# Gateloop attention and a gated feed-forward on one core: the last steps of the range check placed among the last unit's output products

## The chip, the cores and the metric

The kernel runs on one core of a Trainium2 chip. The metric is the device time of one execution, in microseconds (us); the time shown is the median of three runs.

## The reference

Four batches, eight heads, 768 time steps, 48 channels a head. The first block is a recurrence over time with a complex gate; its result goes straight into a feed-forward block with 384 inputs, 2,048 hidden channels and 384 outputs, for 3,072 tokens.

```python
mag = np.sqrt(a_re * a_re + a_im * a_im)
scale = np.minimum(mag, 0.999) / (mag + 1e-06)
for t in range(S):
    new_re = ar * S_re - ai * S_im
    new_im = ar * S_im + ai * S_re
    kv = np.einsum('bhd,bhe->bhde', k[:, :, t], v[:, :, t])
    S_re, S_im = (new_re + kv, new_im)
    y[:, :, t] = np.einsum('bhd,bhde->bhe', q[:, :, t], S_re)
...
h = x @ w_in
sp = np.maximum(h, 0.0) + np.log1p(np.exp(-np.abs(h)))
out = (h * erf(sp)) @ w_out
```

## The kernel before

The work is cut into twelve units of 256 tokens (two chunks `c` of 128). For each unit the kernel takes logarithms and angles of the gates, sums them over time by a product with a triangular matrix, turns and scales `k` and `q`, forms scores and results of the recurrence, and sends the result through the feed-forward: `h` by products with `w_in` (L1178), a copy of `h` by ScalarE (L1181), softplus as a chain of exponentials and logarithms on ScalarE (L786, L787; L786 loads a function table), the Gelu and four VectorE instructions of `erf_times_h` (L1207 to L1213), and the output products (L1271). The weights arrive as 64-bit numbers and are narrowed by VectorE at the start (L844 to L849); later the same weights are loaded a second time and only looked at for small values (`look`, L859).

From the fourth unit on, the output product is done by a scheme with seven products in place of eight (`ff_out_7`). For a unit it makes the products X, Y, Z and W in this order; VectorE first builds sums of `h` (L1224, L1226, L1282, L1286) and of the weights (`sums_of_weights`, L894), and then reads each product into the output tile (L1279, L1291). After Z is read, the rows of the second half of the unit are stored (`put`, L1238), and after W the rows of the first half. Both stores are issued on SP's queue.

This fast way of computing, `quotient_path`, is only valid inside limits. So the kernel collects sums, maxima and minima while it runs, and `check` turns them into one number `ok`. `check` has three steps: the column sums on VectorE (L1337 to L1340), a small product on TensorE that adds over the 128 partitions (L1343), and six comparisons with limits and their minimum on VectorE (L1347, L1348). Then every engine loads `ok` into a register and branches over a second, general path (`product_path`) if it is 1:

```python
        yield
        within = const.tile([1, n], FP, name="within")
        for i, limit in enumerate(LIMITS):
            vector.tensor_scalar(out=within[:, i:i + 1], in0=ps[0:1, i:i + 1], scalar1=limit, scalar2=None, op0=OP.is_le)
        vector.tensor_reduce(out=ok, in_=within, axis=mybir.AxisListType.X, op=OP.min)
...
        fine = nc.values_load(ok[0:1, 0:1], min_val=0, max_val=1)
        with tc.If(fine < 1, label="general"):
            product_path(tc, q, k, v, a_re, a_im, w_in, w_out, out)
```

The load is L1424, the branch L1425. What every engine does after the branch is put down to L1425 and L1452: it checks that its own work is done, SP checks all the DMAs and then all engines, and a closing handshake follows.

The order of the work is written out by hand. `ORDER` is a list of 2,277 names; each name is a generator, and each time the name stands in the list its next step is issued (`next(steps[nm])`), on whichever engine's queue that step belongs to. Each engine works through its own queue in order. The names that this text speaks of: `t`, `l`, `m` the gates' logarithms, `e11.1.4` the steps of `erf_times_h` for unit 11, slab 1, channels 4 and 5 (Gelu, then the four VectorE instructions of which the last writes `h`), `b` sums of the weights, `i` the second look at the weights, `K` and `Q` the turning of `k` and `q`, `f` sums of `h`, `O11.0` to `O11.13` the output products of unit 11 with their reads and stores (`O11.4` and `O11.5` end X, `O11.7` ends Y, `O11.11` ends Z, `O11.13` ends W), and `Z` the three steps of `check`.

Of the kernel before, what the change touches and what calls it, by code (L numbers as in the profile page):

```python
# [49 lines left out]
u4_18 u4_2 u8_0 g0.0 g0.0 g0.1 g0.1 H u4_19 m0.0 m0.0 m0.0 m0.1 m0.1 t0.0 t0.0 l0.0 l0.0 l0.0 l0.0 m0.1 l0.0 p0.0  # L50
t0.1 t0.1 l0.1 l0.1 l0.1 p0.0 p0.0 u2_22 u8_1 n0 t0.0 t0.1 o0.1 l0.1 l0.1 o0.0 r0.0 n0 n0 n0 a0.0 a0.0 a0.0
u2_41 u2_34 q0.0 Q0.0 n1 n1 n1 r0.1 s0.0 s0.0 s0.0 Q0.0 u2_21 u2_39 a0.1 p0.1 u2_40 qT0.0.0 qT0.0.1 k0.0 K0.0
K0.0 kT0.0.0 kT0.0.1 u4_38 g1.0 t1.0 a0.1 g1.0 t1.0 p0.1 m1.0 qT0.0.1 m1.0 qT0.0.0 a0.1 p0.1 s0.1 s0.1 s0.1
u2_20 t1.0 kT0.0.0 kT0.0.1 o1.0 r1.0 n1 A0.0.0 A0.0.1 g1.1 m1.1 p0.0 A0.0.0 q0.1 Q0.1 v0.0 A0.0.1 n3 n3 S0.0
m1.0 a1.0 l1.0 Q0.1 qT0.1.0 k0.1 a1.0 K0.1 qT0.1.0 l1.0 p0.1 p0.0 S0.0 g1.1 qT0.1.1 qT0.1.1 l1.0 m1.1 K0.1 Y0.0
n3 l1.0 a1.0 l1.0 n3 kT0.1.0 kT0.1.1 n2 m1.1 kT0.1.0 A0.1.0 n2 p1.0 A0.1.0 t1.1 kT0.1.1 t1.1 Y0.0 t1.1 l1.1 p1.0
l1.1 p1.0 s1.0 l1.1 s1.0 s1.0 q1.0 v0.1 A0.1.1 A0.1.1 l1.1 n2 Q1.0 o1.1 l1.1 n2 r1.1 Y0.1 Y0.1 Q1.0 S0.1 S0.1 n4
n4 n4 p0.1 S0.1 n4 p1.1 p1.1 g2.1 g2.0 m2 g2.0 g2.1 m2 m2 n6 n6 k1.0 K1.0 qT1.0.0 qT1.0.0 qT1.0.1 a1.1 a1.1 p1.1
a1.1 t2 v1.1 K1.0 l2 t2 l2 h0.0.6 h0.0.6 l2 q1.1 t2 n6 Q1.1 p1.0 n7 n6 n7 k1.1 n5 g3.0 o2 l2 h0.0.4 h0.0.4 n7 l2
# [5 lines left out]
K2.0 Y1.0 Y1.1 t3 t3 S1.1 Y1.0 h1.0.0 K2.0 o3 S1.1 n10 K2.0 S1.1 S2.0 l3 h0.1.4 l3 r3 a3.0 l3 l3 n10 h1.0.2 S2.0  # L65
n12 l3 a3.0 a3.0 p2.0 S2.0 g4.0 g4.0 k2.1 K2.1 n10 g4.1 K2.1 q3.0 g4.1 M2.0 a3.1 a3.1 x0.0 h1.0.0 x0.0 e0.0.2
n12 e0.0.0 p3.1 p3.0 p3.1 p3.1 h1.1.0 M2.0 h1.0.2 M2.0 M2.0 p3.0 Q3.0 e0.0.0 n15 q3.1 v2.1 a3.1 e0.0.2 e0.0.0 m4
p3.0 h1.1.0 t4 e0.0.2 e0.0.0 e0.0.2 K2.1 a3.1 a3.1 Q2.1 g5.1 M2.1 p3.0 M2.1 k3.0 M2.1 p3.1 M2.1 p3.0 h1.1.6
e0.0.4 e0.0.4 h1.1.6 e0.0.6 e0.0.6 e0.0.4 e0.0.6 e0.0.4 m4 m4 e0.0.4 h0.1.2 A2.0.0 A2.0.1 n12 e0.0.6 n12 e0.0.6
A2.0.0 h0.1.2 s3 s3 s3 Q3.0 n15 K3.0 n14 k3.1 h1.0.4 x0.1 t4 x0.1 l4 x0.1 l4 h1.0.4 n15 K3.0 h1.0.6 x0.1 l4  # L70
A2.0.1 t4 n15 l4 O0.1 O0.0 O0.2 O0.4 O0.6 O0.3 A2.1.0 A2.1.0 A2.1.1 A2.1.1 e0.1.2 o4 l4 K3.0 e0.1.2 e0.1.0
e0.1.0 h1.0.6 r4 h1.1.4 h1.1.4 e0.1.2 Y2 Y2 Y2 a4.0 v3.0 e0.1.0 e0.1.2 a4.0 e0.1.0 e0.1.2 e0.1.0 e0.1.6 e0.1.6
e0.1.4 e0.1.4 e0.1.6 e0.1.4 Q3.0 e0.1.4 Q3.1 n14 h1.1.2 h1.1.2 a4.0 a4.0 a4.0 e0.1.6 Q3.1 K3.1 g5.1 x1.0 x1.0
p3.1 n13 x1.0 g5.0 g5.0 M3.0 a4.1 O0.5 O0.7 p4.0 h2.0.2 S3.0 e0.1.4 S3.0 n14 a4.1 n14 n13 e0.1.6 p4.0 p4.0 x1.0
v4.1 n13 n13 O0.9 O0.8 p4.1 p4.1 e1.0.0 h2.0.2 e1.0.0 e1.0.0 e1.0.2 e1.0.2 e1.0.0 e1.0.2 e1.0.0 e1.0.2 e1.0.2
k4.0 q4.0 v4.0 M3.0 a4.1 h2.1.2 M3.0 M3.0 O0.11 m5 h2.1.2 a4.1 m5 m5 K3.1 Q3.1 K3.1 h2.0.6 e1.0.4 h2.0.6 e1.0.4
e1.0.6 e1.0.6 e1.0.4 e1.0.6 l5 t5 p4.1 l5 t5 t5 l5 e1.0.4 Q4.0 p4.1 p4.1 M3.1 M3.1 M3.1 M3.1 q4.1 v3.1 x1.1
h2.0.0 h2.0.0 x1.1 O0.10 A3.0.1 A3.0.0 O0.13 O0.15 O0.12 O0.15 p4.0 p4.0 O0.15 h2.0.4 e1.0.6 e1.0.6 o5 e1.0.4
O0.14 l5 l5 A3.0.1 A3.0.0 l5 x1.1 O0.14 O1.0 x1.1 l5 a4.1 a5.0 A3.1.0 A3.1.0 A3.1.1 A3.1.1 e1.1.0 e1.1.0 e1.1.0
e1.1.2 e1.1.2 e1.1.2 j e1.1.2 e1.1.0 e1.1.2 e1.1.0 s4 s4 s4 Q4.0 r5 a5.0 O1.2 O1.4 O1.1 O1.6 e1.1.6 e1.1.6  # L80
e1.1.4 e1.1.4 e1.1.4 e1.1.6 e1.1.6 e1.1.4 e1.1.4 Y3 Y3 Y3 h2.0.4 x2.0 x2.0 a5.0 x2.0 h2.1.4 h2.1.4 x2.0 S3.1
h2.1.0 O1.3 K4.0 K4.0 K4.0 e1.1.6 S3.1 a5.0 S3.1 Q4.0 Q4.1 Q4.1 O1.8 S4.0 S4.0 S4.0 k4.1 K4.1 O0.14 M4.0 M4.0
e2.0.2 e2.0.2 M4.0 e2.0.0 e2.0.0 e2.0.2 M4.0 e2.0.0 v5.1 e2.0.2 p5.0 p5.0 p5.0 h2.1.6 h2.1.6 e2.0.2 e2.0.0
e2.0.0 e2.0.4 h2.1.0 e2.0.4 e2.0.4 e2.0.6 e2.0.6 e2.0.6 e2.0.6 O1.10 O1.12 a5.0 a5.0 a5.0 K4.1 p5.1 O1.14 p5.1
x2.1 x2.1 O1.5 O1.7 O1.9 K4.1 e2.0.4 a5.1 a5.1 p5.1 x2.1 Q4.1 a5.1 a5.1 A4.0.1 A4.0.1 e2.0.6 x2.1 A4.0.0 h3.0.2
# [9 lines left out]
e3.1.0 M5.1 M5.1 p6.1 O2.10 O2.12 p6.0 p6.1 p6.0 O2.15 p6.1 h4.0.0 h4.0.0 p6.0 e3.1.4 e3.1.4 O2.14 p6.1 g7.1  # L95
g7.1 p6.0 g7.0 b6 s6 e3.1.6 e3.1.4 e3.1.6 e3.1.6 Q6.0 e3.1.4 b2 b0 b2 b2 e3.1.6 g7.0 i0 M5.1 h4.0.4 h4.0.4 O2.14
i1 q6.1 s6 h4.1.6 s6 h4.1.6 m7 m7 m7 b0 l7 t7 l7 A5.0.1 A5.0.1 e3.1.6 Q6.0 i0 b4 e3.1.4 f3.1 b4 h4.0.6 h4.0.2 l7
l7 b4 i1 h4.0.2 h4.0.6 t7 b0 x4.0 A5.0.0 A5.0.0 A5.1.1 O3.0 O3.1 O3.2 h4.1.2 A5.1.0 h4.1.4 O3.3 x4.0 l7 l7 x4.0
x4.0 b2 b6 K6.0 K6.0 O3.1 O3.6 t7 b6 o7 A5.1.0 A5.1.1 Y5 l7 a7.0 e4.0.2 e4.0.2 e4.0.0 e4.0.0 e4.0.2 e4.0.2
e4.0.0 e4.0.2 e4.0.0 h4.1.2 r7 e4.0.0 e4.0.6 O3.2 e4.0.6 h4.1.4 k6.1 v6.0 O2.15 e4.0.4 e4.0.4 e4.0.6 e4.0.4 f3.1  # L100
h4.1.0 Y5 Y5 h4.1.0 O2.14 K6.0 e4.0.6 Q6.0 e4.0.4 x4.1 x4.1 x4.1 M6.0 M6.0 v7.1 M6.0 M6.0 O3.4 O3.5 O3.5 O3.5
O3.5 a7.0 e4.0.6 e4.0.4 a7.0 x4.1 h5.0.6 O3.7 O3.7 Q6.1 O3.7 a7.0 h5.0.2 Q6.1 K6.1 O3.4 e4.1.0 O3.8 e4.1.0 O3.12
a7.0 a7.0 a7.0 a7.1 v7.0 p6.0 e4.1.2 e4.1.2 e4.1.0 e4.1.0 e4.1.2 e4.1.0 e4.1.2 p7.1 h5.0.6 p7.1 p7.1 e4.1.2
e4.1.4 O3.9 O3.10 e4.1.6 p7.0 p7.0 p7.0 h5.0.2 e4.1.4 e4.1.4 e4.1.6 e4.1.6 O3.13 A6.0.1 O3.11 A6.0.0 O3.13 g8.0
# [4 lines left out]
A6.1.1 A6.1.1 h5.1.0 e5.0.4 e5.0.6 e5.0.6 e5.0.6 Q7.0 e5.0.4 Q7.0 O4.4 e5.0.6 e5.0.4 e5.0.6 e5.0.4 e5.0.4 h5.1.0  # L109
K7.0 h5.1.6 l8 l8 h5.1.6 l8 l8 l8 v6.1 Y6 Y6 x5.1 v8.0 x5.1 Y6 x5.1 l8 x5.1 O4.6 O4.7 S6.1 O4.7 O4.7 K7.0 K7.0  # L110
Q7.0 q7.1 Q7.1 l8 Q7.1 O4.12 O4.13 p7.0 p7.0 p6.1 h6.0.2 h6.0.0 O4.13 S6.1 S6.1 O4.8 O4.9 k7.1 p7.1 O4.10 O4.11
e5.1.0 K7.1 e5.1.0 e5.1.2 e5.1.2 e5.1.0 e5.1.0 e5.1.2 e5.1.0 e5.1.2 e5.1.2 r8 e5.1.4 e5.1.4 e5.1.4 h6.0.2 e5.1.6
e5.1.6 e5.1.6 p8.1 p8.1 p8.1 p8.0 p8.0 M7.0 a8.0 a8.0 h6.0.4 M7.0 M7.0 M7.0 A7.0.0 O5.0 g9.1 i4 e5.1.4 p8.0 a8.0
a8.0 e5.1.6 O4.11 a8.0 f5.0 h6.0.0 a8.0 a8.0 e5.1.6 O4.13 e5.1.4 f5.1 i4 a8.1 a8.1 i5 O4.11 g9.0 h6.0.6 h6.0.4
h6.0.6 x6.0 a8.1 S7.0 K7.1 K7.1 Q7.1 a8.1 i5 h6.1.0 x6.0 h6.1.0 x6.0 q8.0 x6.0 S7.0 f5.1 S7.0 A7.0.0 O5.1 O5.2
A7.0.1 O5.2 O5.1 A7.0.1 Q8.0 e6.0.2 e6.0.2 e6.0.0 e6.0.0 a8.1 a8.1 a8.1 e6.0.0 e6.0.2 e6.0.0 e6.0.2 e6.0.2
e6.0.0 M7.1 M7.1 h6.1.4 h6.1.4 g9.1 g9.0 m9 m9 h6.1.6 h6.1.6 s8 O5.3 M7.1 M7.1 q8.1 h6.1.2 h6.1.2 p8.0 p8.0
e6.0.4 A7.1.0 m9 A7.1.0 A7.1.1 e6.0.6 A7.1.1 e6.0.6 e6.0.6 e6.0.4 e6.0.4 O5.4 O5.5 O5.5 O5.5 f5.0 O5.5 s8 s8
Q8.0 x6.1 l9 e6.0.6 Q8.1 Q8.0 Q8.1 e6.0.4 e6.0.4 k8.0 K8.0 Y7 Y7 Y7 O5.4 O5.6 k8.1 S7.1 O5.7 O5.7 K8.0 O5.7
O5.12 O5.13 O5.13 h7.0.0 O5.8 h7.0.6 O5.9 O5.10 O5.11 K8.0 M8.0 l9 x6.1 l9 x6.1 x6.1 l9 M8.0 e6.1.0 S7.1 e6.0.6  # L120
S7.1 l9 K8.1 e6.1.0 e6.1.0 e6.1.2 e6.1.2 e6.1.2 e6.1.0 e6.1.2 e6.1.0 t9 e6.1.2 l9 l9 h7.0.0 e6.1.6 e6.1.4 e6.1.6
O6.0 e6.1.4 e6.1.6 e6.1.4 t9 t9 o9 p9.0 p9.0 e6.1.4 e6.1.6 f6.0 e6.1.4 p9.0 h7.0.6 r9 a9.0 a9.0 p9.1 M8.0 M8.0
e6.1.6 Q8.1 i6 i6 p9.1 i7 p9.1 A8.0.1 h7.0.4 h7.0.4 h7.0.2 a9.0 a9.0 h7.0.2 S8.0 a9.0 v9.1 K8.1 f6.1 f6.1 i7
k9.0 a9.1 a9.1 O5.11 A8.0.1 K8.1 f6.0 O5.11 x7.0 x7.0 a9.1 x7.0 a9.1 O6.3 h7.1.4 h7.1.4 x7.0 h7.1.6 O6.1 a9.1
a9.1 S8.0 O6.1 S8.0 a9.1 g10.0 O5.13 M8.1 g10.1 g10.0 M8.1 g10.1 e7.0.2 p9.1 M8.1 M8.1 e7.0.4 s9 h7.1.6 K9.0
e7.0.2 e7.0.4 e7.0.2 e7.0.4 e7.0.4 e7.0.4 e7.0.2 O6.2 O6.2 O6.4 O6.4 h7.1.2 s9 s9 m10 e7.0.2 K9.0 A8.0.0 h7.1.0
O6.5 O6.6 e7.0.6 O6.5 e7.0.6 m10 O6.5 m10 A8.0.0 O6.5 e7.0.0 e7.0.0 e7.0.0 e7.0.6 q9.0 v8.1 A8.1.0 O6.7 O6.7
A8.1.1 A8.1.1 O6.7 A8.1.0 e7.0.0 e7.0.0 e7.0.6 Q9.0 Q9.0 O6.8 O6.9 O6.10 t10 h7.1.2 l10 h7.1.0 l10 x7.1 t10 x7.1
l10 x7.1 Y8 Y8 Y8 l10 p9.0 p9.0 k9.1 x7.1 v9.0 O6.11 O6.12 t10 e7.0.6 o10 Q9.0 K9.0 l10 K9.1 f7.0 O6.11 M9.0
O6.11 M9.0 M9.0 S9.0 K9.1 e7.1.0 e7.1.0 e7.1.0 e7.1.2 e7.1.2 e7.1.2 l10 h8.0.6 e7.1.0 e7.1.0 e7.1.2 e7.1.2  # L130
h8.0.6 e7.1.4 O7.1 q9.1 e7.1.6 h8.0.0 h8.0.0 l10 e7.1.4 e7.1.4 e7.1.6 e7.1.6 r10 a10.0 Q9.1 a10.0 S9.0 M9.0 i8
O6.13 O6.13 a10.0 e7.1.6 e7.1.6 e7.1.4 e7.1.4 a10.0 f7.1 Q9.1 i8 h8.1.2 h8.1.2 i9 h8.0.2 k10.0 O7.1 p10.1 p10.1
p10.1 h8.0.2 p10.0 p10.0 p10.0 p10.0 h8.0.4 h8.0.4 a10.0 a10.0 a10.0 a10.1 g11.1 K9.1 Q9.1 i9 a10.1 O7.2 O7.2
# [3 lines left out]
A9.1.1 e8.0.4 A9.1.1 e8.0.4 O7.7 O7.7 e8.0.4 e8.0.6 e8.0.6 e8.0.6 e8.0.4 t11 m11 t11 h8.1.0 m11 m11 Q10.0 Q10.0  # L137
# [6 lines left out]
p11.1 h9.1.4 x9.0 x9.0 a11.1 h9.1.2 x9.0 a11.1 h9.1.2 x9.0 S10.0 f8.1 O8.0 O8.1 O8.1 O8.3 A10.0.0 A10.0.0 h9.1.6  # L144
a11.1 a11.1 q11.0 p11.0 e9.0.2 a11.1 e9.0.0 s11 s11 s11 A10.1.0 A10.1.0 A10.1.1 A10.1.1 e9.0.2 O8.2 O8.6 e9.0.0
e9.0.2 e9.0.2 O8.2 e9.0.0 e9.0.2 e9.0.0 e9.0.0 e9.0.6 e9.0.6 e9.0.6 e9.0.4 v10.1 Y10 Y10 Y10 e9.0.4 O8.4 O8.5
# [14 lines left out]
e11.0.2 e11.0.6 e11.0.6 f10.1 e11.0.2 h11.1.0 O10.3 h11.1.4 O10.4 O10.4 O10.5 O9.13 h11.1.0 x11.1.0 x11.1.0  # L161
h11.1.4 x11.1.0 x11.1.1 x11.1.0 e11.1.2 e11.1.0 x11.1.1 x11.1.1 x11.1.1 O10.6 O10.7 O10.5 O10.5 O10.5 O10.7
O10.7 O10.12 O10.8 e11.1.2 e11.1.2 e11.1.2 e11.1.0 e11.1.2 e11.1.0 e11.1.0 e11.1.0 O10.9 O10.10 O10.11 O10.11
f11.0 O10.11 O10.13 O10.13 O10.13 e11.1.4 e11.1.4 e11.1.6 e11.1.6 O11.0 e11.1.4 e11.1.6 O11.1 e11.1.4 e11.1.6
O11.1 O11.3 e11.1.6 e11.1.4 f11.1 f11.0 i15 i15 O11.4 O11.2 O11.6 O11.2 i15 O11.5 Z f11.1 O11.5 Z O11.5 O11.5
O11.4 O11.7 O11.7 O11.7 O11.8 O11.9 O11.10 O11.11 O11.11 O11.11 O11.12 O11.13 O11.13 O11.13 Z
"""
# [1289 lines left out]
```

## Time and profile before

| | us |
|---|---|
| median of three runs (659.18 to 659.3) | 659.18 |
| the profiled execution | 659.41 |
| its span in the profile | 657.6 |
| W's last product on TensorE ends | 650.7 |
| VectorE's read of W starts, lasts | 650.78, 0.36 |
| the six comparisons together; the minimum | 0.46; 0.15 |
| the profiled TensorE clock | 0.998 of full |

A span begins with the first and ends with the last instruction that the profiler recorded; the rest of an execution's time lies around it. The profile calls TensorE PE (its weight loads PEld), VectorE DVE, ScalarE ACT, GpSimd POOL and SyncE SP; a q behind an engine's name is its sequencer, which loads registers, waits, branches and issues DMAs. Rows of instructions give their start, their length and, in brackets, how long the engine idled before and what ended the idling. GpSimd computes only in the first two microseconds of this path; SP issues the DMAs.

### The profile page before, as it was taken

To read this page: it belongs to the slowest core of one execution; us is meant where nothing else is said; L and a number is where in the kernel's file an instruction comes from. 1 tells how busy PE (TensorE), PEld (TensorE's weight loads), DVE (VectorE), ACT (ScalarE), POOL (GpSimd) and SP (SyncE) were. 2 spreads that over 40 slices of the span, in tenths; PEclk is the share of its full clock that TensorE was granted. 3 is DMA by queue.
4 is the path that set the end of the run, shared out by engine and by line. 5 is a ranking of instruction groups with operands and counts; after the bars stand their busy time and mean duration, and the time that the engine had idled before them with its cause. 6 is when DMAs were issued, how large, how long until landed. Compare 5 with 4: busy or idle time off the path is not lost.

```text
span 657.6 us, 12344 instructions
## 1 busy us (share of the span) xinstructions
PE 640.9 (97%) x4728; PEld 564.0 (86%) x4728; DVE 598.3 (91%) x976; ACT 583.8 (89%) x768; POOL 1.1 (0%) x8
## 2 busy tenths in 40 slices
PE   8999999999999999999999999999999999999995
PEld 7778887777778768999999998999998999999985
DVE  7999999999989899999999899899999899967992
ACT  6999999999999999998997999996998893788730
POOL 0000000000000000000000000000000000000000
PEclk9999999999999999999999999999999999999999
DMA  8998965743352437248446535726725707500020
GB/s 204 223 246 216 203 136 120 147 67 58 68 106 56 85 61 168 50 70 193 79 63 173 89 50 133 145 50 155 131 41 111 143 14 177 111 2 25 1 73 27
DMA packets 282792, 70.19 MB, mean 107 GB/s; under 512 B 269396, under 2 KB 272488, under 8 KB 282728
## 3 DMA queue, kind: packets, MB, share of 16 engines
q1 hardware_dynamic: 282728, 69.36, 49.6%
q8 instruction: 38, 0.62, 0.4%
q14 instruction: 26, 0.21, 0.1%
HBM read 48.82 MB, written 4.75 MB: 81 GB/s over the span
## 4 chain that ended last, share of the span: by engine, by line
ACT 40%; PE 28%; DVE 21%; issue 5%; DMA 3%; SPq 2%; DVEq 0%; ACTq 0%
PE hps L1178 13%; ACT L786 10%; ACT yy L787 7%; ACT z L787 6%; ACT e L787 4%; PE Y L1271 3%; ACT CS L787 2%; DVE yy L1209 2%; DVE z L1207 2%; PE X L1271 2%; DVE h L1213 2%; DVE e L1211 2%; ACT y L787 2%; PE Z L1271 2%; PE sc L1106 2%
## 5 line engine op out<-in xcount | busy, mean ns | idle before, releaser
L1178 PE MATMUL hps<-xT,w_in_sb 128*128 128x256 f32 x1152 | 261.8, 381 | 0.1
L1178 PEld LDWEIGHTS hps<-xT,w_in_sb 128*128 128x128 f32 x1152 | 215.4, 190 | 31.9 <-ACT h L1181 2.4
L786 ACT ACT_TABLE_LOAD x98 | 125.7, 1283 | 2.5 <-PEq L1441 0.9
L1207 DVE TENSOR_TENSOR z<-z,yy 128x512 f32<-128x512 f32 x96 | 64.3, 686 | 18.5 <-ACT e L787 18.0
L787 ACT ACTIVATE e<-z 128x512 f32<-128x512 f32 x96 | 57.4, 625 | 16.0 <-DVE h L1213 15.4
L1213 DVE SCALAR_TENSOR_TENSOR h<-e,h 128x512 f32<-128x512 f32 x96 | 64.8, 685 | 1.3
L1209 DVE SCALAR_TENSOR_TENSOR yy<-z,yy 128x512 f32<-128x512 f32 x96 | 64.5, 688 | 1.4
L1211 DVE TENSOR_TENSOR e<-e,yy 128x512 f32<-128x512 f32 x96 | 64.8, 684 | 0.8
L1247 PE MATMUL ops<-w_out_sb,h 128*128 128x384 f32 x192 | 64.9, 487 | 0.1
L1181 ACT COPY h<-hps 128x512 f32<-128x512 f32 x96 | 55.1, 577 | 9.9 <-PE hps L1178 9.9
L1247 PEld LDWEIGHTS ops<-w_out_sb,h 128*128 128x128 f32 x192 | 36.0, 190 | 22.1 <-DVE w_out_sb L849 0.5
L1106 PEld LDWEIGHTS sc<-KQ 96*128 96x128 f32 x384 | 47.4, 192 | 6.2 <-issue 1.6
L1106 PE MATMUL sc<-KQ 96*128 96x128 f32 x384 | 49.0, 276 | 2.7 <-DVE qt L1069 1.0
L787 ACT ACTIVATE z<-h 128x2048 f32<-128x2048 f32 (+1 forms) x25 | 46.1, 1844 | 5.7 <-DVE found L859 4.2
L787 ACT ACTIVATE z<-z 128x2048 f32<-128x2048 f32 (+1 forms) x25 | 46.0, 1842 | 0.5
L787 ACT ACTIVATE yy<-z 128x2048 f32<-128x2048 f32 (+1 forms) x25 | 46.0, 1839 | 0.3
L787 ACT ACTIVATE yy<-yy 128x2048 f32<-128x2048 f32 (+1 forms) x25 | 46.0, 1839 | 0.2
L1110 DVE TENSOR_TENSOR KQ<-sc,triu 128x512 f32<-128x512 f32 x48 | 32.2, 682 | 0.8 <-PE sc L1106 0.8
L1125 PEld LDWEIGHTS kv<-v,kt 128*96 128x96 f32 x320 | 29.8, 165 | 2.9 <-ACT xT L1167 0.7
L1164 PE MATMUL y<-KQ,v 128*32 128x128 f32 x768 | 31.5, 274 | 0.0
L1125 PE MATMUL kv<-v,kt 128*96 128x48 f32 x320 | 30.0, 247 | 0.6 <-ACT xT L1167 0.4
L1271 PE MATMUL X<-T,S 128*128 128x192 f32 x144 | 25.4, 327 | 1.2 <-DVE S L1282 1.2
(122 smaller groups left out, 1057.5 us busy)
## 6 DMA issues: line engine op xcount, KB each, us to landing
KQ<-X SPq DMA_DIRECT2D x240, 64.0 KB
raw<-in_moe_w_in_dram SPq DMA_DIRECT2D x8, 768.0 KB
raw<-in_moe_w_out_dram SPq DMA_DIRECT2D x8, 768.0 KB
again<-in_moe_w_in_dram SPq DMA_DIRECT2D x8, 768.0 KB
ar<-in_a_re_dram SPq DMA_DIRECT2D x24, 192.0 KB
ai<-in_a_im_dram SPq DMA_DIRECT2D x24, 192.0 KB
q<-in_q_dram SPq DMA_DIRECT2D x24, 192.0 KB
k<-in_k_dram SPq DMA_DIRECT2D x24, 192.0 KB
```

The lines of the kernel that those rows point to most:

```text
L786: scalar.preload_act_table_set(sets[0])
L787: scalar.activation(func=func, **kw)
L1106: nc.tensor.matmul(out=ps[:, j, :], lhsT=head("k", g * HG + j, u, c), rhs=head("q", g * HG + j, u, c), start=True, stop=True)
L1125: nc.tensor.matmul(out=kv[0:D2, j, :], lhsT=T["kt", u, c][:, j].rearrange("p u d -> p (u d)"), rhs=side(T["v", u][:, c, j // 2], j % 2), s ...
L1178: nc.tensor.matmul(out=ps[:, e, :], lhsT=w_in_sb[:, (sl * SLAB + i) // 2, kd, e * P:(e + 1) * P], rhs=T["xT", u][:, kd, :], start=(kd == 0 ...
L1181: scalar.copy(out=T["h", u, sl][:, i:i + 2, :], in_=ps)
L1207: vector.tensor_tensor(out=z, in0=z, in1=y, op=OP.mult)
L1209: vector.scalar_tensor_tensor(out=y, in0=z, scalar=-2.0, in1=y, op0=OP.add, op1=OP.mult)
L1211: vector.tensor_tensor(out=e, in0=e, in1=y, op=OP.mult)
L1213: vector.scalar_tensor_tensor(out=h, in0=e, scalar=1.0 / RT2, in1=h, op0=OP.add, op1=OP.mult)
L1247: nc.tensor.matmul(out=ps, lhsT=lhsT, rhs=w_out_sb[:, i, :], start=i == HALF, stop=i == KF - 1)
L1271: nc.tensor.matmul(out=ps, lhsT=a(sl)[:, i], rhs=b(sl, i), start=sl == 0 and i == 0, stop=sl == NSL - 1 and i == HALF - 1)
```

## The change

Only `ORDER` is edited. The same 2,277 names stand in it, each as often as before. At its end the third step of `Z` (the comparisons and the minimum) moves from the last place to just behind `O11.7`, ahead of `O11.8` to `O11.13`; the second step (the product) moves by one place, to before the third `O11.5`. Also near the end, the two stores of unit 10 (the last steps of `O10.13` and `O10.11`) move behind the first step of `i15`, a load, and `O11.3` (part of X) moves ahead of `O11.1`'s second step. Further up, other names change places with near neighbours, 97 in all; the places below are the first, those around 123, 255, 421, 436, 482, 582 and 594 us of the profile before, and the end.

```diff
-u4_18 u4_2 u8_0 g0.0 g0.0 g0.1 g0.1 H u4_19 m0.0 m0.0 m0.0 m0.1 m0.1 t0.0 t0.0 l0.0 l0.0 l0.0 l0.0 m0.1 l0.0 p0.0
-t0.1 t0.1 l0.1 l0.1 l0.1 p0.0 p0.0 u2_22 u8_1 n0 t0.0 t0.1 o0.1 l0.1 l0.1 o0.0 r0.0 n0 n0 n0 a0.0 a0.0 a0.0
+u4_18 u4_2 u8_0 g0.0 g0.0 g0.1 g0.1 H u4_19 m0.0 m0.0 m0.0 m0.1 m0.1 t0.0 t0.0 t0.1 l0.0 l0.0 l0.0 l0.0 m0.1 l0.0
+p0.0 t0.1 l0.1 l0.1 l0.1 p0.0 p0.0 u2_22 u8_1 n0 t0.0 t0.1 o0.1 l0.1 l0.1 o0.0 r0.0 n0 n0 n0 a0.0 a0.0 a0.0
 ...
-e0.1.4 e0.1.4 e0.1.6 e0.1.4 Q3.0 e0.1.4 Q3.1 n14 h1.1.2 h1.1.2 a4.0 a4.0 a4.0 e0.1.6 Q3.1 K3.1 g5.1 x1.0 x1.0
+e0.1.4 e0.1.6 e0.1.4 Q3.0 Q3.1 n14 e0.1.4 h1.1.2 h1.1.2 a4.0 a4.0 a4.0 e0.1.6 Q3.1 K3.1 g5.1 x1.0 x1.0 p3.1 n13
 ...
-g7.1 p6.0 g7.0 b6 s6 e3.1.6 e3.1.4 e3.1.6 e3.1.6 Q6.0 e3.1.4 b2 b0 b2 b2 e3.1.6 g7.0 i0 M5.1 h4.0.4 h4.0.4 O2.14
-i1 q6.1 s6 h4.1.6 s6 h4.1.6 m7 m7 m7 b0 l7 t7 l7 A5.0.1 A5.0.1 e3.1.6 Q6.0 i0 b4 e3.1.4 f3.1 b4 h4.0.6 h4.0.2 l7
+g7.1 p6.0 g7.0 b6 s6 e3.1.6 b2 e3.1.6 e3.1.4 e3.1.6 Q6.0 b0 b0 e3.1.4 b2 b2 e3.1.6 g7.0 i0 M5.1 h4.0.4 h4.0.4
+O2.14 i1 q6.1 s6 h4.1.6 s6 h4.1.6 m7 m7 m7 l7 t7 l7 A5.0.1 A5.0.1 e3.1.6 Q6.0 i0 e3.1.4 b4 f3.1 b4 h4.0.6 h4.0.2
 ...
-e7.0.2 e7.0.4 e7.0.2 e7.0.4 e7.0.4 e7.0.4 e7.0.2 O6.2 O6.2 O6.4 O6.4 h7.1.2 s9 s9 m10 e7.0.2 K9.0 A8.0.0 h7.1.0
+e7.0.2 e7.0.4 e7.0.2 e7.0.4 e7.0.4 e7.0.2 e7.0.2 O6.2 O6.2 e7.0.4 O6.4 O6.4 h7.1.2 s9 s9 m10 K9.0 A8.0.0 h7.1.0
 ...
-l10 x7.1 Y8 Y8 Y8 l10 p9.0 p9.0 k9.1 x7.1 v9.0 O6.11 O6.12 t10 e7.0.6 o10 Q9.0 K9.0 l10 K9.1 f7.0 O6.11 M9.0
+l10 x7.1 x7.1 Y8 Y8 Y8 l10 p9.0 p9.0 k9.1 x7.1 v9.0 O6.11 O6.12 t10 o10 e7.0.6 K9.0 l10 K9.1 f7.0 O6.11 M9.0
 ...
-A9.1.1 e8.0.4 A9.1.1 e8.0.4 O7.7 O7.7 e8.0.4 e8.0.6 e8.0.6 e8.0.6 e8.0.4 t11 m11 t11 h8.1.0 m11 m11 Q10.0 Q10.0
+A9.1.1 e8.0.4 A9.1.1 e8.0.4 O7.7 O7.7 e8.0.4 e8.0.6 e8.0.6 e8.0.6 t11 m11 t11 h8.1.0 m11 Q10.0 m11 e8.0.4 Q10.0
 ...
-e10.0.2 O9.7 A11.1.1 A11.1.1 A11.1.0 A11.1.0 O9.8 i14 v11.1 e10.0.2 e10.0.0 e10.0.0 e10.0.2 O9.7 O9.7 h10.1.0
+e10.0.2 A11.1.1 A11.1.0 A11.1.1 O9.8 A11.1.0 i14 v11.1 e10.0.2 e10.0.0 e10.0.2 O9.7 O9.7 e10.0.0 O9.7 h10.1.0
 ...
-e10.1.0 e10.1.0 h11.0.4 h11.0.4 h11.0.6 e10.1.2 h11.0.6 i14 e10.1.2 e10.1.4 h11.0.2 e10.1.4 e10.1.2 e10.1.4
+e10.1.0 h11.0.4 h11.0.4 h11.0.6 e10.1.2 h11.0.6 i14 e10.1.0 e10.1.2 e10.1.4 h11.0.2 e10.1.4 e10.1.2 e10.1.4
 ...
-e11.0.2 e11.0.6 e11.0.6 f10.1 e11.0.2 h11.1.0 O10.3 h11.1.4 O10.4 O10.4 O10.5 O9.13 h11.1.0 x11.1.0 x11.1.0
+e11.0.6 e11.0.6 e11.0.2 e11.0.2 h11.1.0 O10.3 h11.1.4 O10.4 O10.4 f10.1 O10.5 O9.13 h11.1.0 x11.1.0 x11.1.0
 ...
-O10.7 O10.12 O10.8 e11.1.2 e11.1.2 e11.1.2 e11.1.0 e11.1.2 e11.1.0 e11.1.0 e11.1.0 O10.9 O10.10 O10.11 O10.11
-f11.0 O10.11 O10.13 O10.13 O10.13 e11.1.4 e11.1.4 e11.1.6 e11.1.6 O11.0 e11.1.4 e11.1.6 O11.1 e11.1.4 e11.1.6
-O11.1 O11.3 e11.1.6 e11.1.4 f11.1 f11.0 i15 i15 O11.4 O11.2 O11.6 O11.2 i15 O11.5 Z f11.1 O11.5 Z O11.5 O11.5
-O11.4 O11.7 O11.7 O11.7 O11.8 O11.9 O11.10 O11.11 O11.11 O11.11 O11.12 O11.13 O11.13 O11.13 Z
+O10.7 O10.12 O10.8 e11.1.2 e11.1.2 e11.1.2 e11.1.0 e11.1.2 e11.1.0 e11.1.0 e11.1.0 O10.9 O10.10 O10.11 f11.0
+O10.11 O10.13 O10.13 e11.1.4 e11.1.4 e11.1.6 e11.1.6 O11.0 e11.1.4 e11.1.6 e11.1.4 e11.1.6 e11.1.4 O11.3 O11.1
+O11.1 e11.1.6 f11.1 f11.0 i15 O10.13 O10.11 i15 O11.4 O11.2 O11.6 i15 O11.2 O11.5 Z f11.1 Z O11.5 O11.5 O11.5
+O11.4 O11.7 O11.7 O11.7 Z O11.8 O11.9 O11.10 O11.11 O11.11 O11.11 O11.12 O11.13 O11.13 O11.13
```

## The prediction

> **What bounds the kernel now.** I read the totals first, then the chain of waits, then the last 18 us instruction by instruction, because the change names the end of the queues.
>
> ```profile
> PE 640.9 (97%) x4728; PEld 564.0 (86%) x4728; DVE 598.3 (91%) x976; ACT 583.8 (89%) x768; POOL 1.1 (0%) x8
> ACT 40%; PE 28%; DVE 21%; issue 5%; DMA 3%; SPq 2%; DVEq 0%; ACTq 0%
> ```
>
> No engine alone is the limit. The chain goes through TensorE (PE), VectorE (DVE) and ScalarE (ACT) in turn, all about 90% busy, so a gain of one engine in the body only counts where the other two can follow. The end is different. These are the last pieces of the chain of waits (start, length, what):
>
> ```profile
> 642.85 5.29 PE Z L1271 x32
> 648.14 2.61 PE W L1271 x16
> ...
> 650.78 0.36 DVE out L1279
> 651.13 0.39 DVE within L1347 x6
> 651.55 0.15 DVE ok L1348
> ```
>
> PE is through with W at 650.75, DVE reads it, and only then come the seven small instructions that make `ok` (ready at 651.70). Yet the span is 657.6. The missing 5.9 us have no busy engine; they show only when one asks for the instructions of the branch by line (engine, operation, count, ns min/median/max, first and last start):
>
> ```profile
> L1424 SPq TENSOR_LOAD <-ok x1: 750/750/750, 651.7 to 651.7; - x1
> L1424 POOLq TENSOR_LOAD <-ok x1: 792/792/792, 651.7 to 651.7; - x1
> ...
> L1425 SPq EVENT_SEMAPHORE  x8: 17/17/17, 653.4 to 653.9; - x8
> L1425 ACTq COMPARE_BRANCH  x1: 68/68/68, 652.5 to 652.5; - x1
> L1425 POOLq COMPARE_BRANCH  x1: 59/59/59, 652.6 to 652.6; - x1
> ...
> L1425 SPq COMPARE_BRANCH  x1: 70/70/70, 652.9 to 652.9; - x1
> L1425 ACTq EVENT_SEMAPHORE  x1: 17/17/17, 653.0 to 653.0; - x1
> ...
> L1425 POOLq EVENT_SEMAPHORE  x1: 17/17/17, 656.7 to 656.7; - x1
> ...
> L1452 SPq DRAIN  x3: 7/7/7, 656.7 to 657.1; - x3
> ...
> SPq L1452 <- POOLq L1425: 2.2, 1, 2.2
> ```
>
> Every engine loads `ok` into a register, branches over the skipped path and goes on. ACT needs 0.5 us from its branch to its next instruction (652.5 to 653.0), SP the same, DVE and PE about 0.6. POOL needs 4.1 us (652.6 to 656.7), and SP, which gathers the others, waits 2.2 us for it. So **the end of the span is set by POOL's branch, and that by `ok`**: 651.7 + 0.9 to the branch + 4.1 + 0.9 of closing handshake = 657.6.
>
> **The tail.** In the build after the change DVE's order is: both reads of Y, the six comparisons and the minimum, the read of Z, the read of W. SP's is: the load of `ok` and its two checks, the last two stores, the branch. PE's is unchanged at the end; the small product already stood among the output products (641.2). "The product" of the title needs no cost: what moves is its readers.
>
> - *Removed behind W:* 651.70 - 651.14 = 0.56 us of DVE. Alone that is all a count of instructions would give.
> - *Added before Z:* the same seven. Y's second read ends at 643.13 + 0.94 = 644.07; they last 651.70 - 651.05 = 0.65 us; `ok` is there at 644.7. The wait they bring, for the product, ended at 641.3 and is covered by 2.7 us. Behind them on DVE stand only the reads of Z and W, and SP's two stores behind those. DVE idles 4.1 us before the read of Z (end of PE's Z, 648.14), so the seven are hidden; were that cover gone, Z's store would be 0.65 us late.
> - *SP:* load, two checks and no branch end near 644.7 + 1.2 = 645.9; the first store behind them starts at 648.76. Slack 2.9 us; free. Each store is one DMA, as before.
> - *POOL:* 644.7 + 0.9 + 4.1 = 649.7, under PE's last products. Its 4.1 us go off the path.
> - *What is late next:* SP. W's store is issued as before at 651.16, 0.34 us, to 651.50. SP branches at 651.6, stands at its checks at 652.1, and passes them some 0.07 us apart (eight from 653.4 to 653.9, eight more from 654.0). One of the first eight is W's store, whose landing the trace has at 653.03; the data still moved at 652.4 and not after 652.8. From there one check and the eight of the barrier, 0.6 us, reach 653.7. DVE loads `ok` behind its read of W: 651.14 + 0.9 + 0.6 = 652.7, earlier. PE is earlier still.
> - *Closing handshake:* 656.7 to 657.57, 0.85 us, as it is. New end 653.7 + 0.85 = 654.55.
>
> Sum of the tail: 657.57 - 654.55 = **3.0 us less**.
>
> [...] The row says: four engines cross the branch in 0.5 to 0.6 us, one in 4.1. [...] By the row SP pays 0.5 and the gain is 3.0. I take the row: SP, ACT, DVE and PE crossed the same branch to the same place in this trace. All five give the branch hint at 0.8 us; POOL has almost nothing between hint and branch, which the change leaves so. [...]
>
> **The body.** The list of steps is more than a moved tail: 97 of 2,277 steps stand elsewhere, nearly all by one to five places. No work is added. Setting the two queues of each engine side by side, I looked for idle time ahead of the moved instructions:
>
> ```profile
> 6.03 0.52 ACT L787 ACTIVATE s<-s 128x384 f32<-128x384 f32 x1 [1.24 <-DVE s L933]
> ...
> 258.24 1.13 PE L1106 MATMUL sc<-KQ 96*128 96x128 f32 x8 [1.02 <-DVE qt L1069]
> ...
> 482.07 0.96 DVE L940 TENSOR_TENSOR s<-s,y 128x768 f32<-128x768 f32 x1 [0.49 <-ACT y L787]
> ...
> 594.97 0.63 ACT L787 ACTIVATE e<-z 128x512 f32<-128x512 f32 x1 [1.68 <-DVE h L1213]
> ```
>
> (1) At 6.0 a logarithm of the second chunk (0.51, less 0.07 of overlap) is put into ACT's idle 1.24 us: -0.44. Its operand's DMA is read by DVE at 5.92, so it may come too late for all of it: 0 to -0.44. (2) Near 255 one step of the weights' sums (L894) leaves the way from `s` to `qt`, 0.47, and 0.11 of it comes back ahead of `s`: PE's scores start 0.36 sooner. (3) At 482 `qt` (0.87) goes into an idle of 0.49 while `e` (0.60) comes behind `s`: -0.27 for the transpose. (4) At 594.9 a reduction (0.47) goes ahead of the `h` that ACT waits for; ACT had a gap of 0.17 later, and 0.2 stays: +0.2. (5) The scale reduction ahead of S near 638.7 fills DVE's idle of 0.60; PE is not waiting for it: 0. (6) Near 630 PE's X goes ahead of Y and DVE puts `h` before S; Y still waits for the sum that ends at 637.0: 0. (7) The load of the last weight piece now stands ahead of unit 10's two stores on SP; both were early by microseconds: 0. (8) The other swaps lie inside stretches where PE runs without a gap (74 to 126, 258 to 290, 346 to 371, 537 to 596) or change places on a queue whose sum is unchanged: 0 each, with an error of up to one instruction (0.5 to 0.9).
>
> Sum -0.9. Between 14 and 120 DVE shows under 2 us of idle, and PE is 97% busy, so I let half through: **-0.4**; ends +1.2 and -1.6.
>
> Total -3.4. The profiled execution took 659.41, of which 657.57 is span and 1.84 lies around it: 659.41 - 3.4 = 656.0. The three timed runs have a median of 659.18, 0.23 below the profiled one; I predict for them 659.18 - 3.4 = **655.8**.
>
> **Rivals.**
>
> - *The body gives all it has* (-0.9 to -1.6): 654.6 to 655.3. For it: three of the moves fill a named idle. Against: gains on a queue that feeds two others at 90% get lost. Chance 0.14.
> - *The long branch moves to SP*, or to DVE or PE: tail 0, with the body 658.8, no measurable change. [...] Against: SP's 0.5 us. Chance 0.08.
> - *The body loses on ACT's wait for `h`*, and that is the other side. ACT waits 15.4 us in all, 12 times, for DVE's `h` (it frees the buffer of `e`). Six swaps put `e` or `h` later, by 0.94 (near 123), 0.6 (421), 0.94 (436), 2.0 (481), 0.46 (582), 0.46 (594), together 5.4 us. If all reached ACT, 5.4 - 3.0 = +2.4: 661.6. It decides from 3.0 us on, that is if more than half arrive. Against: at 123 and 582 PE sets the pace, at 421 the second `h` is not later, and only the one at 594 stands before an ACT that waits. Chance 0.06.
> - *The forecast*, tail -3.0 and body within a microsecond: 0.72, own range 654.8 to 657.0.
>
> **Numbers.** Range 653.9 to 657.6: below, the body's best; above, the body's +1.2 and a part of SP paying. 0.2% is 1.3 us, about what a measurement here can tell from nothing. Faster 0.87 (forecast, first rival, a little of the second), within 0.08, slower 0.05.
>
> **What would show it.** POOL's branch near 645.6 and its next instruction near 649.7, before PE ends; SP no longer waiting for POOL; SP's branch to its checks 0.5 us; from the end of W's read to the end of the span 3.4 us in place of 6.4. Wrong if the last PE product ends later than 651, or if SP's or DVE's first instruction past the branch is 4 us behind it.

## The result, and the profile after

The changed kernel takes 656.35 us (median of five runs, 655.93 to 657.28); before, run beside it, takes 659.3 (659.18 to 660.92). The ratio is 0.9951, with a 95% interval of 0.9937 to 0.9966: about 3.2 us (2.2 to 4.2) less. The forecast was 655.8, range 653.9 to 657.6.

The profiled execution is the longest of the five, 657.28, of which 655.5 is span. First its page, the totals, the clock row and the shares of the chain of waits:

```profile
PE 642.5 (98%) x4728; PEld 565.4 (86%) x4728; DVE 598.1 (91%) x976; ACT 584.2 (89%) x768; POOL 1.1 (0%) x8
...
PEclk9989999999999999999999999999999999999999
...
ACT 43%; DVE 23%; PE 21%; DMA 5%; issue 5%; SPq 3%; DVEq 0%; POOL 0%; ACTq 0%; POOLq 0%
```

The counts of instructions are those of before; the change only moves them. New is the 8 in the clock row, of which more below. The last products in the chain of waits (start, length):

```profile
643.88 5.29 PE Z L1271 x32
649.17 2.61 PE W L1271 x16
```

W ends at 651.77, which is 1.03 *later* than before (650.74), and still the span ends 2.0 earlier. The gain lies behind W's end. The instructions of the branch by line (engine, operation, count, ns, first and last start):

```profile
L1424 POOLq TENSOR_LOAD <-ok x1: 494/494/494, 645.7 to 645.7; - x1
...
L1425 SPq EVENT_SEMAPHORE  x8: 17/17/17, 653.1 to 654.2; - x8
...
L1425 POOLq COMPARE_BRANCH  x1: 59/59/59, 646.3 to 646.3; - x1
...
L1425 POOLq EVENT_SEMAPHORE  x1: 17/17/17, 648.9 to 648.9; - x1
...
L1425 SPq COMPARE_BRANCH  x1: 70/70/70, 652.6 to 652.6; - x1
```

GpSimd branches at 646.3 and goes on at 648.9, while TensorE is still at Z. SP branches at 652.6 and stands at its checks 0.52 later. What SP's queue waited for in the last 16 us (us in total, times, longest):

```profile
SPq L1425 <- SPq L1425: 1.1, 2, 0.6
SPq L1452 <- PEq L1452: 0.6, 2, 0.4
```

The row of before in which SP waits 2.2 for POOL is gone. From the end of W's read to the end of the span it is 3.37 in place of 6.43: 3.06 less.

Of the 3.06, this one execution gave 1.03 back earlier. The windows of the first 45 us show where (window, length, busy PE, PEld, DVE, ACT, POOL, then granted clock, DMA share, GB/s):

```profile
34.70:38.10 3.40, 2.35 (x39) 2.03 (x30) 3.40 (x6) 3.35 (x7) 0.00 (x0) 1.00 0.96 223
38.10:41.60 3.50, 3.50 (x12) 2.40 (x12) 3.36 (x6) 3.28 (x6) 0.00 (x0) 0.51 1.13 272
```

For 3.41 us TensorE ran at half clock, right after it had idled 1.05. Before has the same idle, and its clock stays at 1.00. Its second window:

```profile
38.10:41.60 3.50, 3.50 (x17) 2.59 (x18) 3.36 (x6) 3.49 (x6) 0.00 (x0) 1.00 1.12 294
```

ScalarE's first copy of `h` slips from 45.64 to 46.56, and about a microsecond of that stays to the end. Four of the five timed runs have a mean clock of 0.999 or 1.0 where the profiled one has 0.997; they took 655.93 to 656.65. So it varies from execution to execution of the same kernel; it also comes in executions of other versions, below.

### The profile page after: what moved, and what is told of

It reads as the page before. It is cut to its first block, busy times and chain, and to the rows that moved or that the text cites. A ratio compares the mean times of both kernels' runs of the same rounds, so it can differ in the third digit from the quotient of the medians.

```text
span 655.5 us, 12345 instructions
## 1 busy us (share of the span) xinstructions
PE 642.5 (98%) x4728; PEld 565.4 (86%) x4728; DVE 598.1 (91%) x976; ACT 584.2 (89%) x768; POOL 1.1 (0%) x8
## 4 chain that ended last, share of the span: by engine, by line
ACT 43%; DVE 23%; PE 21%; DMA 5%; issue 5%; SPq 3%; DVEq 0%; POOL 0%; ACTq 0%; POOLq 0%
ACT L786 10%; PE hps L1178 8%; ACT yy L787 8%; ACT z L787 6%; ACT e L787 4%; DVE yy L1209 3%; DVE z L1207 3%; DVE e L1211 3%; DVE h L1213 3%; ACT CS L787 3%; SPq L1086 2%; ACT th L787 2%; PE Y L1271 2%; ACT y L787 2%; ACT h L1181 2%
## 5 line engine op out<-in xcount | busy, mean ns | idle before, releaser
L787 ACT ACTIVATE e<-z 128x512 f32<-128x512 f32 x96 | 57.6, 626 | 15.9 <-DVE h L1213 15.2
L1213 DVE SCALAR_TENSOR_TENSOR h<-e,h 128x512 f32<-128x512 f32 x96 | 64.9, 685 | 1.1
```

Of the source, the lines that this page charges most:

```text
L787: scalar.activation(func=func, **kw)
L1213: vector.scalar_tensor_tensor(out=h, in0=e, scalar=1.0 / RT2, in1=h, op0=OP.add, op1=OP.mult)
```

## The experiments

The word *crossing* stands for the time from the start of an engine's branch to its next instruction, *tail* for the time from the end of W's read to the end of the span, *last `h`* for the start of VectorE's last L1213, which ends the body. All were run with the kernel before on the same chip, and ratios are against that; a gain is worked out from the medians where it says so.

**Tail alone.** Before, with one name moved, the third `Z`. (The second `Z` stays where it is, before the third `O11.5`; in the change it stands before the second.)

```diff
-O11.4 O11.7 O11.7 O11.7 O11.8 ... O11.13 O11.13 O11.13 Z
+O11.4 O11.7 O11.7 O11.7 Z O11.8 ... O11.13 O11.13 O11.13
```

> The kernel before with one name moved: the third step of the check stands behind the third O11.7, as after the change; the other 96 moves are left out. Theory 1 (the whole gain is POOL's branch leaving the path): the body is untouched, W's last product ends near 650.7 as before, POOL crosses its branch before that, from the end of W's read to the end of the span 3.3 to 3.5 in place of 6.4; time 3.0 to 3.1 below before, 656.1 to 656.3. Theory 2 (the other 96 moves give a part): the gain is clearly less than that of the whole change, under 2.6. Theory 3 (only the seven instructions behind W count): 0.56 less, 658.6.

```profile
L1425 POOLq COMPARE_BRANCH  x1: 59/59/59, 645.5 to 645.5; - x1
...
L1425 POOLq EVENT_SEMAPHORE  x1: 17/17/17, 648.3 to 648.3; - x1
```

GpSimd is through at 648.3, and the tail is 3.33, so 3.10 shorter than before: that is the shortening of the whole change. In time the ratio is 0.9961 (0.9947 to 0.9975), median 656.99 against 659.55: 2.6 less (1.6 to 3.5). Theory 3 falls. The time alone does not part Theory 1 from Theory 2, whose limit of 2.6 it just meets; the next version does.

**Body alone.** The changed kernel with that name put back at the end (the diff above, reversed).

> The changed kernel with the third step of the check put back at the very end; the other 96 moves stay. Theory 1: POOL is again last, its branch lies after W's read and takes 4 us, from the end of W's read to the end of the span 6.4 as before; what is left is the body alone, between 0 and 0.4 less than before, 658.8 to 659.2. Theory 2 (the moves in the body share the gain): 0.6 to 1.6 less than before. Theory 3 (they cost time, hidden in the result by a larger gain of the tail): above before by 0.3 or more.

```profile
SPq L1452 <- POOLq L1425: 2.0, 1, 2.0
```

Ratio 1.0007 (0.9996 to 1.0019): 0.5 more, from 0.3 less to 1.3 more. The tail is 6.19, and SP waits 2.0 for POOL again. No gain in the body is seen, and one above 0.3 is excluded; both Theory 2s fall, and a small loss (Theory 3) is neither shown nor excluded.

**The changed kernel once more**, for the runs beside it.

> The changed kernel once more, as the measure for the runs beside it. Theory (tail 3.0, body nothing): 3.0 to 3.2 below before. In an execution whose clock is not halved near 38 the last h of VectorE lies within 0.3 of before (635.3 to 635.9), and the span is near 654.2; in one where it is, 1.0 to 1.2 later.

Ratio 0.9958 (0.9945 to 0.9972); tail 3.33. The clock is at 1.0 in the profile until W, but the last `h` is not within 0.3 of before: this execution is 0.02 later at 509 and 0.59 later at 528. At 513.4 VectorE waits 0.88 for the second load of the output weights, where it waited 0.27 before. A load that takes a few tenths longer or shorter moves the body by as much as all its moves were to gain. The order of before shows the same spread: in the trace of the tail alone the last `h` starts at 635.90 in place of 635.59, and in the three single runs below (two of them with memsets added on GpSimd) 0.5 to 1.6 later than before, all at full clock near 38.

**Who pays at the branch: the hint.** Whether SP owes its 0.52 to the hint that it gives at 0.8 us can be tested by taking the hint away. First the changed kernel, with SP left out of it:

```diff
-engines = [... for e in ("PE", "DVE", "SP", "Activation", "Pool")]
+engines = [... for e in ("PE", "DVE", "Activation", "Pool")]
```

> The changed kernel with SyncE left out of the engines that give the branch hint at the start (TensorE, VectorE, ScalarE and GpSimd still give it). [...] Theory 2 (the hint plays no part in SP's crossing): 0.5 as it was, no change in time.

Ratio 0.9983 (0.997 to 0.9996), median 658.25 where the tail alone, on the same chip, has 656.99: half the gain is lost. SP at the branch in this version:

```profile
L1425 SPq EVENT_SEMAPHORE  x8: 17/17/17, 654.2 to 654.7; - x8
...
L1425 SPq COMPARE_BRANCH  x1: 45/45/45, 651.5 to 651.5; - x1
```

SP now crosses in 2.72 in place of 0.52. The tail is 5.03, only 1.7 longer, as SP no longer waits for the landing of W's store at its checks; the time is 1.3 longer than that of the tail alone. About 1.05 after the branch the trace has two DMA packets of 8,192 bytes on a queue named "instruction". So Theory 2 falls: **SP's short crossing is what the hint gives**, 0.52 with it and 2.72 without.

Then why does GpSimd, which has the hint, pay? Before, with 300 memsets of one element on GpSimd, issued behind its first work:

```diff
             next(steps[nm])
+        idle = const.tile([1, 1], FP, name="idle")
+        for _ in range(300):
+            nc.gpsimd.memset(idle, 0.0)
```

> The kernel before (check at the end) with 300 memsets of one element on GpSimd behind its own work of the first 2 us. [...] Theory 2 (GpSimd pays whatever is behind its hint): 4 us, no change. [...]

```profile
L1428 POOLq COMPARE_BRANCH  x1: 65/65/65, 654.3 to 654.3; - x1
...
L1428 POOLq EVENT_SEMAPHORE  x1: 17/17/17, 654.8 to 654.8; - x1
```

The crossing falls to 0.48 (L1428 is the same line as L1425, moved by the edit). Ratio 0.997 (0.996 to 0.9981), 1.9 less in the medians, with the check still at the very end; tail 4.16. So Theory 2 falls. The 1.9 is a little under the 2.2 that SP had waited for GpSimd before, and the profiled execution had the half clock near 38. Three versions separate hint and length. They have one run each, and the run of before beside them, 661.11, has a mean clock of 0.995 where the page of before has 0.998; so they are read by crossing and tail, not by time. Without GpSimd's hint, queue as it was:

> The kernel before without the branch hint on GpSimd. Theory 1 (GpSimd's hint has no effect as long as its queue is a dozen instructions): its crossing is 3.8 to 4.1 as before, and so is the time. Theory 2 (the hint helps GpSimd a little, and without it the crossing would be longer): 5 or more, and the time 1 longer or more.

Crossing 4.05, tail 6.39, against 4.09 and 6.43 with the hint: on this short queue it made no difference. With the 300 memsets, without the hint:

> The 300 memsets on GpSimd at the start, check at the end as before, but no branch hint on GpSimd. Theory 1 (the 0.48 with 300 memsets came from the hint being acted upon on the way through the longer queue): the crossing is 2.6 to 4.1 again. Theory 2 (a longer queue alone makes the crossing short, for instance because the code behind it lies otherwise): 0.5 without the hint.

Crossing 4.13, tail 6.46. The length alone made no difference either; the 0.48 came with both. With the hint and only 60 memsets:

> As with 300 memsets, hint included, but only 60 of them. [...] Theory 2 (a few microseconds of work behind the hint are enough): 0.5, and 2 less in time.

Crossing 0.50, tail 4.18 (time 658.71): Theory 2. A packet of 8,192 bytes on the queue named "instruction" stands at 9.1 us in this trace, when about 50 of the 60 have run, and before has none until 28.0. The 300 memsets without the hint have one too, at 10.8, so it comes with the longer queue and not with the hint. What this packet has to do with the hint is not shown; how many instructions it takes, between a dozen and about 70, was not tried.

**How late may `ok` come?** Before, with the check between the reads of Z and W:

```diff
-O11.10 O11.11 O11.11 O11.11 O11.12 O11.13 O11.13 O11.13 Z
+O11.10 O11.11 O11.11 O11.11 Z O11.12 O11.13 O11.13 O11.13
```

> The kernel before with the third step of the check between the reads of Z and of W, so that ok is ready near 649.4. Theory 1 (the end is the later of two chains: ok plus the load, POOL's crossing and the handshake; or W's store, SP's branch and the handshake): POOL would be through at 649.4 + 0.9 + 2.7 to 4.1 = 653.0 to 654.4, the span ends between 653.8 and 655.2; time 2.4 to 3.0 less than before. If POOL's crossing is 4.0 here as before, the gain is near the lower figure, and SP's sequencer waits about 0.6 for POOL; if 2.7 as after the change, the gain is that of the whole move, 3.0. Theory 2 (what counts is how many instructions stand behind W on VectorE): 0.56 less, as any place before W's read would give.

Ratio 0.9978 (0.9968 to 0.9989), 1.1 less in the medians: between the theories. (The tail is 2.1 shorter; by difference some 1.0 is lost in the body of these executions, whose order is that of before. The profiled one has the half clock near 38, and its last `h` is 1.7 later.) The profile does not fit Theory 1's account:

```profile
L1425 SPq EVENT_SEMAPHORE  x8: 17/17/17, 653.8 to 655.8; - x8
L1425 POOLq COMPARE_BRANCH  x1: 59/59/59, 651.9 to 651.9; - x1
L1425 SPq COMPARE_BRANCH  x1: 70/70/70, 653.3 to 653.3; - x1
L1425 POOLq EVENT_SEMAPHORE  x1: 17/17/17, 654.5 to 654.5; - x1
```

GpSimd is through at 654.5, and SP stands at its eight checks until 655.8. It waits for W's store, which lands 2.83 after its issue; in the versions above that is 1.84 to 1.90. Tail 4.30. Five "instruction" packets of 8,192 bytes and one of 16,384 run between 652.9 and 655.6, beside the store. To see whether GpSimd's are to blame, the same with 60 memsets, so that it crosses in 0.5:

> The check between Z's and W's reads, with the 60 memsets on GpSimd. Theory 1 (in the version without memsets W's store was late, 2.83 from issue to landing in place of 1.87, because GpSimd's fetch of its target's code ran beside the store): GpSimd crosses in 0.5, its fetches at the end are gone, the store lands 1.85 to 1.90 behind its issue, and from the end of W's read to the end of the span it is 3.3 to 3.4 in place of 4.30; time about 3.0 below before. Theory 2 (something else held the store back, as TensorE's fetch of 16384 bytes): still 2.5 to 2.9 to the landing, 4.0 to 4.3 to the end.

GpSimd crosses in 0.50, but the store still takes 2.58 and the tail is 4.06; ratio 0.9968 (0.9958 to 0.9979). Theory 1 falls: GpSimd's crossing is not the cause. A packet of 16,384 bytes and four of 8,192 still run beside the store.

The packets and landings of the traces point to the large one. W's store has 128 packets of data and sixteen landings, so one for eight packets. In the version without memsets fifteen come by 1.87 from the store's issue, as in the others. Eight packets start only from 1.49 on, as the packet of 16,384 bytes ends (0.24 to 1.50), and the sixteenth landing is the one at 2.83. With the memsets the large packet runs from 0.25 to 1.36; three landings come at 1.96 to 2.16 and the last at 2.58. In the versions with 1.84 to 1.90 the large packet is through before the store's data move or starts after they have, while two packets of 8,192 bytes at the end of the data (without SP's hint: from 1.43) do no harm. In every version the last large packet starts 1.1 to 2.0 after TensorE's branch, so it is most likely TensorE's; no version with only TensorE's branch moved was run.

**Two additions that could beat the change.** Eight unread products on TensorE fill the idle time near 37 us:

```diff
-n4 n4 p0.1 S0.1 n4 p1.1 p1.1
+n4 n4 p0.1 S0.1 n4 u8_50 p1.1 p1.1
```

> The changed kernel with eight unread TensorE products (128 x 128, 0.11 each) ahead of the running sum that TensorE waits 1.05 for near 37. Theory 1 (that idle time is what now and then halves the clock for 3.41, which costs about 1.2): no halving near 38 in any execution, so the slow ones go, the median falls by 0.3 to 0.8 against the changed kernel and the spread narrows; the lowest time stays. Theory 2 (the halving has another cause): still there in some executions, no change. If the products delay the sum: 0.1 to 0.2 more.

Ratio 0.9951 (0.9937 to 0.9965), median 656.14 against 656.45 for the changed kernel beside it. No halving in five runs, but that has none on this chip either, so the test does not decide. And, on top of the eight products, with the last store cut in two:

```diff
             put(u, 1)
+            if u == 11:
+                nc.sync.dma_start(out=out[u * C * P:u * C * P + P, HD:], in_=part(1))
...
-            put(u, 0)
+            if u == 11:
+                nc.sync.dma_start(out=out[u * C * P:u * C * P + P, :HD], in_=part(0))
+            else:
+                put(u, 0)
```

> The same with the last store cut: the 192 columns of the first rows that are final after Z's read are stored then, and only the other 192 after W's. Theory 1 (the time from the last store's issue to its landing, 1.90, goes with its bytes): landing 0.2 to 0.35 after its issue sooner, and the time less by as much. Theory 2 (it goes by the packets, 128 in either case, and a fixed part): 0 to 0.1.

The store lands 1.64 after its issue, not 1.85, and the tail is 3.05 in place of 3.33: Theory 1, by 0.2 to 0.3. Ratio 0.9941 (0.9928 to 0.9955), median 655.49. That is 0.65 below the eight products alone, from which the cut store is the only difference, and 0.96 below the changed kernel (656.45); both are more than the tail accounts for, and the intervals overlap. It has the lowest ratio here.

## Why the prediction was right, and where it was not

**The tail, -3.0, was right as a whole.** It measured -3.06 in the profile of the change and -3.10 in that of the tail alone, and the signs named for it came: GpSimd through before TensorE ends, SP not waiting for it, SP's crossing 0.5. One sign of being wrong came too: the last product ends later than 651, at 651.77 with the half clock and at 651.24 in the second trace of the change. The limit of 651 was set closer than the body's own spread from execution to execution; the branch has no part in it. The tail's two legs were sized unequally well. SP's leg (the branch, 0.5 to the checks, the landing of the store as the last of them, the handshake) came out within 0.1. GpSimd's leg was given 0.9 for the load and 4.1 for the crossing; it took 0.49 and 2.66. The loads of `ok` last 0.74 to 0.85 when four or five of them run at once, and 0.47 to 0.54 where no more than three do. GpSimd's crossing is 2.59 to 2.83 where its branch comes earlier than SP's and VectorE's, and 3.85 to 4.13 in the four versions where all five branch within 0.3 us and GpSimd has no hint, or has it with only a dozen instructions; why it differs stays open. GpSimd had over four microseconds to spare, so nothing came of the wrong sizes.

**The row.** I took the row, 0.5 for SP, and the result bears it out with 0.52. My reason was the right one only in part: that SP had crossed the same branch to the same place before. I named the hint, and GpSimd's want of instructions behind it, but did not rest the choice on them. What SP's short crossing hangs on here is the hint: without it the crossing is 2.72. The upper end of the range counts in "a part of SP paying", and one rival all of it; no run in which SP has the hint shows that, and in the one without it the tail is 5.03 in place of 3.33.

**The step that failed is "I let half through: -0.4".** No gain of the body was seen (1.0007; its interval ends at 0.3 less), and the tail alone is within its interval of the whole. Measured 3.2 (2.2 to 4.2) is no proof of 3.4 rather than 3.0. Traces without a half clock near 38 show each term. I use the version without SP's hint, whose body is that of the change. It is one pair of traces, and loads that land earlier or later move a body by more than most of these terms; so the pair shows where these gains went here, not what each is worth on average.

(1) The logarithm at 6.0 ran in ScalarE's idle time as foreseen, but had to wait for its operand until 5.71, so VectorE's F starts at 14.22 in place of 14.46: -0.24 of the -0.44. That is gone at 359.5. VectorE there waits for the second load of the input weights, which it did not have to before. The row of before, then that of the version without SP's hint:

```profile
359.38 0.94 DVE L859 TENSOR_REDUCE found<-again 128x1 f32<-128x768 f32 x1
...
359.48 0.95 DVE L859 TENSOR_REDUCE found<-again 128x1 f32<-128x768 f32 x1 [0.47 <-DMA again<-in_moe_w_in_dram]
```

(2) Near 255 `qt` is done 0.63 earlier, at 257.61, more than the -0.36 hoped for. TensorE's scores still start at 258.14, 0.10 earlier, with the body as a whole 0.18 ahead:

```profile
258.14 1.13 PE L1106 MATMUL sc<-KQ 96*128 96x128 f32 x8 [1.08 <-DMA KQ<-X]
```

Where before had "DVE qt" as the releaser, now it is a DMA: a wait took the place of the wait removed, and (2) is worth 0.

(3) At 482 the transpose of `qt` came 0.38 earlier (483.55 against 483.93), more than the 0.27; 0.23 of it is left on VectorE from 492 on. That was given back by 528. About 0.1 of it goes while VectorE waits for the DMA of `s` (516.42 against 516.56 before), the rest on ScalarE, where two logarithms that depend on each other now follow directly. Before (three rows), then without SP's hint:

```profile
517.57 1.89 ACT L787 ACTIVATE yy<-z 128x2048 f32<-128x2048 f32 x1
519.37 0.56 ACT L1181 COPY h<-hps 128x512 f32<-128x512 f32 x1
519.83 1.91 ACT L787 ACTIVATE yy<-yy 128x2048 f32<-128x2048 f32 x1
...
517.43 1.90 ACT L787 ACTIVATE yy<-z 128x2048 f32<-128x2048 f32 x1
519.36 1.91 ACT L787 ACTIVATE yy<-yy 128x2048 f32<-128x2048 f32 x1
```

The second starts 1.93 after the first. Before, a copy of `h` stood between them and started 1.80 after it. So a swap "on a queue whose sum is unchanged", item (8), cost 0.13. (4) did not show: from 552 to 599 us the body moves by -0.07, not +0.2.

Together the last `h` is at 635.53 against 635.59. I had looked for idle time on the engines; in this pair two of the three gains ended at DMAs that no engine's busy time shows.

**Rivals.** "The body gives all" and "the body loses on ACT's wait for `h`" are out: the body alone is between 0.3 less and 1.3 more, and ScalarE's wait for `h` is 15.2 us in the changed kernel, 15.4 before. "The branch moves to SP" did not happen, and without the hint, where it does, 1.3 of gain is left, not the 0.4 given to it.

## What to carry to other kernels

Ask of a tail which engines do nothing there but branch, and start them early: the scalar that decides the branch should be ready some microseconds before the last store (6.5 in the change), not between the reads of the last two products, where a packet of 16,384 bytes ran beside that store and it landed after 2.58 and 2.83 in place of 1.84 to 1.90. On GpSimd a branch hint did something here only with 60 or more instructions put behind it (crossing 0.50, against 4.09 with a dozen); on SP, which branches last, it took 2.2 us off the crossing and 1.3 off the time. Before a gap on an engine's queue is counted as a gain, see whether an operand further on comes by DMA: at 258 and 359 us the gain ended there.

## What had not been expected of the hardware

- GpSimd with a branch hint and a dozen instructions: crossing 3.85 (body alone) and 4.09 (before), against 4.05 without the hint. With the hint and 60 more instructions: 0.50.
- Where the idle time near 37 lies against the stretches of one clock. In the traces of before and of the change these stretches last 3.41, 30.72, 614.40 and 648.53 us, which are 1, 9, 180 and 190 times 3.41. Counted on in steps of 3.41 from the start of such a stretch, in all five profiles with the half clock (the change, the body alone, the 300 memsets with the hint, both versions with the check between the reads) a step ended 0.13 to 0.51 after the idle time; in the seven others that keep the idle time whole it ended 1.25 or more after it, among them four in which all of it lay in one step (the tail alone and the three single runs), as it does in the five. The first full-clock stretch starts at 6.89 before and at 7.43 in the change. Whether this decides the clock, and why it would, is not shown.
- W's store took 1.84 to 1.90 from issue to landing, but 2.58 and 2.83 where a packet of 16,384 bytes on the "instruction" queue ran beside it; in the second, fifteen of its sixteen landings were on time.
